# Attention, expert layer and softplus layer on one core: nine attention steps ahead, the input split among them, and the gate in four column groups

## The chip, the cores and the metric

The kernel runs on one core of a Trainium2 chip. The metric is the device time of one execution in microseconds. PE is the matrix engine, DVE the vector engine, ACT the scalar engine, POOL the general engine, SP the engine that here only issues DMAs. The time before the change is 2075.95 us, the median of 3 runs (2073.23 to 2079.36).

## The reference, cut to what matters

All data is float32.

```python
# q, k, v: (4, 8, 576, 64)
k_p = k.reshape(B, H, 72, 8, D).mean(axis=3)          # pooling over 8 positions
v_p = v.reshape(B, H, 72, 8, D).mean(axis=3)
attn = softmax(q @ k_p.T / sqrt(D));  x = attn @ v_p  # x: (2304, 512) over all heads
P = exp(x @ w_gate - max)                             # w_gate: (512, 8)
for _ in range(8):                                    # rows, then columns, to fixed sums
    P /= P.sum(1, keepdims=True) + 1e-09
    P /= P.sum(0, keepdims=True) + 1e-09
    P *= N / E
out = sum(P[:, e:e+1] * (relu(x @ w1[e]) @ w2[e]) for e in range(8))   # w1: (8, 512, 1024)
h = out @ w_in;  y = softplus(h) @ w_out              # w_in: (512, 2048)
```

## The kernel before

**Attention** goes in 32 steps. A step takes one batch, one half of the positions (W = 288) and one pair of heads; four steps in a row (`hp` 0 to 3) complete the 512 channels of 288 tokens. For a batch and a pair of heads, k and v are pooled once (`pool_kv`: a reduction each on DVE; for the first four pairs POOL adds up v), the pooled keys are transposed (`keys_first`), and they serve two steps. `attn_step(m)` overlaps several steps: it transposes q of step m+1 (`channels_first`), issues scores, maximum and difference of step m (`softmax`), transposes the attention of a step divided earlier (`turn_attn`), lets ACT take the exponent, lets DVE and POOL divide (`divide`; in the early part one step late), multiplies with v (`mix`) and pools. In the early part, step m so transposes and mixes step m-2. The last `mix` of four also computes the gate: 288 tokens by 8 experts, four products over 128 channels each, a copy by ACT and a DMA to `lgd`.

**Experts.** The tokens come in three sets (512, 896, 896 tokens: `PAIRS`), an expert's 1024 hidden units in four blocks of 256, so there are 32 blocks for each token set. A block's first layer (`first_moe`) is a 2x2 block product by seven products of sums, after Strassen and Winograd: `b11`, `t2`, `t1`, `t4`, `t3`, `b21`, `b22` are blocks of the input or differences of such (`t_sums`), `A11` to `S4` those of the weights (`sums_w1`, on POOL). Each operand is split into a rounded part and a remainder (`split_x`, `prep_w1`, `prep_w2`: ACT rounds, POOL or DVE subtracts), and each product is three matrix products (`three`). The second layer (`second`) goes by 128 tokens. The order on each engine is that of the program: first(0), first(1), second(0), first(2), second(1) and so on. The matrices of PSUM come from eight banks that all users take in turn.

**What is put where.** The input of the first token set, 512 tokens, is complete after attention step 7, mixed at step 9. Ten attention steps (`AHEAD`) and then the differences and splits of the input are issued ahead of the first block. In them, the pooling of pairs 4 to 7 stands at steps 3, 5, 7 and 9, the sums of the first weights after step 4 and their split after step 6. The rest of attention is fed in by `hook`, which is called seven times in a `first_moe` and once for every 128 tokens of a `second`; each call is a slot. Every fifth slot, beginning with the second, issues one `attn_step`. When attention is done, the slots take the iterations on P (`side`), then the scaling of the first sums by P (`shares_to_raw`), then the conversion of the last weights from 64 bits (`from_float64`). Before block 20 everything in `side` is flushed.

Two memory pools on the right side, `ld_e` and `at_e`, serve the early steps only; the pools for the hidden layer, `h` and `z`, take their place afterwards. ACT's `za` is the copy of the first product that later sums need. All DMAs are issued by SP, in program order.

Of the kernel before, what the change touches and what calls it, by code (L numbers as in the profile page):

```python
# [9 lines left out]
F32 = mybir.dt.float32  # L10
# [9 lines left out]
def attention_moe_softplus_kernel(  # L20
# [26 lines left out]
    QP = 96  # L47
    JH = S // QP // 2
    W = JH * QP
    G = JH * 2  # L50
    STEPS = B * 2 * HP
    ITERS = 8
# [171 lines left out]
    NQ = 6  # L224
    kbd = [at_p.tile([P, 2 * SP], F32, name=f"kbd{i}", bufs=1) for i in range(NK)]
    next_kv = [0]
    AHEAD = 10
    kv_t = {}
    q_l = {}
    pooled = {}  # L230
# [1 line left out]
    to_divide = []  # L232
    to_turn = []
    to_mix = []
    xb = {}

    def kv_of(m):
# [65 lines left out]
    def softmax(m):  # L303

        ps = bank("s")
        qT = q_t.pop(m)
        kb = kbd[kv_of(m) % NK]
        for j in range(JH):
            nc.tensor.matmul(ps[:QP, j * 2 * SP:(j + 1) * 2 * SP], qT[:, j * QP:(j + 1) * QP], kb)  # L309
        sv = ps[:QP, :G * SP].rearrange("p (g s) -> p g s", g=G)  # L310
        pool = at_e if m < AHEAD and m % 3 == 2 else at_p
        mx = at_p.tile([QP, G], F32, tag="mx", name="mx")
        ex = pool.tile([QP, G, SP], F32, tag="ex", name="ex")
        s1 = ps[:QP, G * SP:G * SP + G]
        nc.vector.tensor_reduce(mx, sv, axis=AX.X, op=ALU.max)
        nc.vector.tensor_tensor(ex, sv, mx.unsqueeze(2).to_broadcast([QP, G, SP]), op=ALU.subtract)

        def exp():
            nc.scalar.activation(ex, ex, AF.Exp)

        def divide():
            sm = at_p.tile([QP, G], F32, tag="sm", name="sm")
            nc.vector.tensor_reduce(s1, ex, axis=AX.X, op=ALU.add)
            nc.vector.tensor_scalar_add(s1, s1, 1e-9)
            nc.vector.reciprocal(sm, s1)
            nc.gpsimd.tensor_tensor(ex, ex, sm.unsqueeze(2).to_broadcast([QP, G, SP]), op=ALU.mult)
            to_turn.append((m, ex))

        return exp, divide
# [11 lines left out]
    def mix():  # L341
        m, aT = to_mix.pop(0)
        hb, hp = divmod(m, HP)
        vp = pooled[kv_of(m)][1]
        px = bank("px")
        for h in range(2):
            nc.tensor.matmul(px[h * D:(h + 1) * D, :W], vp[:, h, :], aT[:, h, :])  # L347

        t0 = hb * W
        here = max(0, min(W, TP0 - t0))  # L350
        x0 = x_of(0)
        if here < W and hp == 0:
            xb[hb] = at_p.tile([P, KC, W], F32, tag="xb", name="xb")
        if here:
            nc.scalar.activation(x0[:, hp, t0:t0 + here], px[:, :here], AF.Copy, scale=1.0 / POOL)
        if here < W:
            nc.scalar.activation(xb[hb][:, hp, :], px[:, :W], AF.Copy, scale=1.0 / POOL)
        if hp == HP - 1:
            if here < W:
                nc.sync.dma_start(xd[:, :, max(0, t0 - TP0):t0 + W - TP0], xb[hb][:, :, here:])  # L360
            pg = bank("pg")
            src = x0[:, :, t0:t0 + W] if here == W else xb[hb]
            for c in range(KC):
                nc.tensor.matmul(pg[:E, :W], wg[:, c, :], src[:, c, :], start=c == 0, stop=c == KC - 1)  # L364
            lg = at_p.tile([E, W], F32, tag="lg", name="lg", bufs=1)
            nc.scalar.copy(lg, pg[:E, :W])
            half, o = divmod(t0, LT * P)
            nc.sync.dma_start(lgd[half, :, o:o + W], lg)


    pool_at = {}
    for i in range(2, B * HP):
        b, hp = divmod(i, HP)
        pool_at.setdefault(hp - 2 if b == 0 else 2 * HP * b - 5 + 2 * hp, []).append(i)
    turn_at = {}
    for m, l in pool_at.items():
        turn_at.setdefault(m + 1, []).extend(l)
    turn_at.setdefault(0, []).append(1)

    def attn_step(m, early):  # L380


        last = STEPS
        if m + 1 < last:
            channels_first(m + 1)
        if m < last:
            exp, divide = softmax(m)
        while to_turn:
            turn_attn()
        for i in turn_at.get(m, ()):  # L390
            keys_first(i)
        if m < last:
            exp()
            to_divide.append(divide)
        while len(to_divide) > (1 if early else 0):
            to_divide.pop(0)()
        while len(to_mix) > (0 if early or m >= last else 1):
            mix()
        for i in pool_at.get(m, ()):
            pool_kv(i)  # L400

    for i, pool in enumerate((ld_e, ld_e, ld_p, ld_p)):
        load_kv(pool)
# [146 lines left out]
    def first_moe(n, between):  # L550

        whi, wlo = w1_t.pop(n)
        at = h_tiles(n)
# [11 lines left out]
        a, u1 = (zpool.tile([P, tb], F32, tag="z", name=x) for x in ("za", "u1"))  # L565
        add = lambda o, x, y: nc.vector.tensor_tensor(o, x, y, op=ALU.add)  # L566
        product(pa, A11, "b11")
        nc.scalar.copy(a, pa)  # L568
        between(0)
        product(pb, S2, "t2")  # L570
        add(u1, pb, a)
        between(1)
        product(pc, S1, "t1")
# [8 lines left out]
        product(pa, A12, "b21", True)  # L582
# [178 lines left out]
    def hook(light=True):  # L761
        slot[0] += 1
        if attn_m[0] is not None:
            if slot[0] % 5 == 2:
                attn_step(attn_m[0], False)
                attn_m[0] += 1
                if attn_m[0] >= STEPS and not to_turn and not to_mix:
# [17 lines left out]
    def shares_to_raw(experts):  # L785

        for e in experts:
            for i in range(TP0 // P):
                def add(i=i, e=e):
                    a, s = acc_of(1, i), prob[:, i, e:e + 1]  # L790
                    if e == 0:
                        nc.scalar.activation(a, a, AF.Copy, scale=s)
                    else:
                        nc.vector.scalar_tensor_tensor(a, raw_of(e, i), s, a, op0=ALU.mult, op1=ALU.add)
                side.extend([add, None, None] if e else [add])

    def load_x(pair):
        o = OFF[pair] - TP0
# [4 lines left out]
        return lambda i: v[:, i]  # L803


    for m in range(AHEAD):
        attn_step(m, True)
        if m == 4:
            sums_w1(0)
        if m == 6:  # L810
            prep_w1(0)
            load_w(1, 1)
    ectx.close()
    hctx = ExitStack()
    hpool = hctx.enter_context(tc.tile_pool(name="h", bufs=2, side="right"))
    zpool = hctx.enter_context(tc.tile_pool(name="z", bufs=2, side="right"))
    tpool = None


    ta = hpool.tile([P, 2, 2, TP0 // 2], F32, tag="hhi", name="ta")  # L820
    tb = hpool.tile([P, 2, 2, TP0 // 2], F32, tag="hlo", name="tb")
    t0_of = lambda i: (ta, tb)[i // 2][:, i % 2]
    first_sums = t_sums(x_of(0), t0_of, on_pool=(2,))
    first_splits = splits("moe", x_of(0), t0_of, on_pool=(2, 4))
    first_sums[0]()
    first_splits[0]()
    for x in first_sums[1:]:
        x()
    for x in first_splits[1:]:
        x()  # L830

# [25 lines left out]
    for step, (what, n) in enumerate(todo):  # L857
# [4 lines left out]
        elif what == "first":  # L862
            f, kind, pair, u = sets[n]
            nxt = sets[n + 1] if n + 1 < len(sets) else None
            if not n or sets[n - 1][0] != f:
                xs.update(xs_next)
                xs_next.clear()
            if nxt is not None and nxt[1] == "moe":
                sums_w1(n + 1)
            if nxt is not None and nxt[0] != f:  # L870

# [30 lines left out]
                load_w(1, n + 2)  # L902
            if todo[step + 1][0] != "second":
                go_on()
                prep_w2(n)
                load_w(2, n + 1)
                while pending:
                    pending.pop(0)()
        else:
# [73 lines left out]
```

## Time and profile before

| | |
|---|---|
| median of 3 runs | 2075.95 us |
| profiled execution | 2079.37 us, its span 2076.7 us |
| PE busy | 2028.2 us, 98% of the span |
| DVE busy | 1456.5 us, 70% |
| POOL busy | 1245.6 us, 60% |
| ACT busy | 836.1 us, 40% |
| mean granted clock of PE | 0.992 of 2.4 GHz |

The profiled execution is one execution, recorded by the hardware; its span reaches from the first to the last instruction, and 2.7 us lie around it. A granted clock of 1.00 is 2.4 GHz; 1.2 GHz is the other level. Matrix products are pipelined, so the records of one after the other overlap, and the distance from start to start is what one costs in a row. A 32-bit product shows as two records, with a weight load each. Names with L are lines of the kernel.

### The profile page before, as it was taken

To read this page: it belongs to the slowest core of one execution; us is meant where nothing else is said; L and a number is where in the kernel's file an instruction comes from. 1 tells how busy PE (TensorE), PEld (TensorE's weight loads), DVE (VectorE), ACT (ScalarE), POOL (GpSimd) and SP (SyncE) were. 2 spreads that over 40 slices of the span, in tenths; PEclk is the share of its full clock that TensorE was granted. 3 is DMA by queue.
4 is the path that set the end of the run, shared out by engine and by line. 5 is a ranking of instruction groups with operands and counts; after the bars stand their busy time and mean duration, and the time that the engine had idled before them with its cause. 6 is when DMAs were issued, how large, how long until landed. Compare 5 with 4: busy or idle time off the path is not lost.

```text
span 2076.7 us, 27725 instructions
## 1 busy us (share of the span) xinstructions
PE 2028.2 (98%) x10285; PEld 1753.6 (84%) x10285; DVE 1456.5 (70%) x2531; ACT 836.1 (40%) x1607; POOL 1245.6 (60%) x1011
## 2 busy tenths in 40 slices
PE   6899999999999999999999999999999999999998
PEld 4677788877888888888888888888888888888897
DVE  7787588776677667777776776777655666767766
ACT  3455544353322332222243223222222365565565
POOL 4666689987555555666555555555555554544555
PEclk9899999999999999999999999999999999999999
DMA  6343223445222332222242222222121211121132
GB/s 178 99 133 108 86 85 109 153 139 178 76 91 82 115 109 77 92 92 82 78 151 86 87 76 77 92 82 92 56 61 61 62 51 51 61 87 51 61 114 75
DMA packets 133762, 192.00 MB, mean 92 GB/s; under 512 B 26924, under 2 KB 82940, under 8 KB 133628
## 3 DMA queue, kind: packets, MB, share of 16 engines
q1 hardware_dynamic: 133628, 190.25, 29.3%
q8 instruction: 80, 1.31, 0.3%
q14 instruction: 54, 0.44, 0.1%
HBM read 166.94 MB, written 23.27 MB: 92 GB/s over the span
## 4 chain that ended last, share of the span: by engine, by line
PE 84%; DVE 7%; ACT 3%; POOL 2%; DMA 2%; issue 2%; SPq 0%; ACTq 0%; DVEq 0%; POOLq 0%
PE py L486 42%; PE p L486 31%; PE ph L486 7%; POOL w1lo L167 1%; PE s L309 1%; PE px L347 1%; DVE c L517 1%; DMA xlod<-xl 1%; DVE kp L267 1%; PE pg L364 1%; POOL w2lo L167 1%; PE pa L337 0%; DVE vp L273 0%; DVE ln L524 0%; DVE c L522 0%
## 5 line engine op out<-in xcount | busy, mean ns | idle before, releaser
L486 PE MATMUL py<-w2hi,hhi 128*128 128x512 f32 x1440 | 566.9, 394 | 4.5 <-DVE g L642 3.2
L486 PE MATMUL py<-w2lo,hhi 128*128 128x512 f32 x1440 | 562.0, 390 | 1.9 <-POOL w2lo L167 1.9
L486 PE MATMUL py<-w2hi,hlo 128*128 128x512 f32 x1440 | 561.9, 390 | 0.0
L167 POOL TENSOR_TENSOR w1lo<-w1raw,w1hi 128x512 fp32r<-128x512 f32 (+1 forms) x216 | 253.4, 1192 | 469.7 <-ACT w1hi L198 383.7
L486 PE MATMUL p<-xhi,w1hi 128*128 128x448 f32 (+1 forms) x1344 | 460.2, 342 | 9.2 <-DVE u L566 2.9
L486 PE MATMUL p<-xhi,w1lo 128*128 128x448 f32 (+1 forms) x1344 | 457.3, 340 | 6.5 <-POOL w1lo L167 6.5
L486 PE MATMUL p<-xlo,w1hi 128*128 128x448 f32 (+1 forms) x1344 | 457.7, 341 | 1.6 <-DVE xlo L439 1.6
L642 DVE SCALAR_TENSOR_TENSOR g<-py,prob,g 128x512 f32<-128x512 f32 x482 | 360.6, 749 | 102.5 <-PE py L486 90.6
L501 ACT ACTIVATE hhi<-p 128x448 fp32r<-128x448 f32 (+1 forms) x384 | 180.4, 494 | 424.7 <-PE p L486 414.4
L167 POOL TENSOR_TENSOR w2lo<-w2raw,w2hi 128x1024 fp32r<-128x1024 f32 x120 | 289.2, 2410 | 62.2 <-ACT w2hi L211 56.7
L486 PEld LDWEIGHTS py<-w2hi,hhi 128*128 128x128 f32 x1440 | 270.7, 188 | 63.3 <-DVE g L642 3.5
L486 PEld LDWEIGHTS py<-w2hi,hlo 128*128 128x128 f32 x1440 | 270.6, 188 | 59.1
L486 PEld LDWEIGHTS py<-w2lo,hhi 128*128 128x128 f32 x1440 | 271.0, 188 | 51.9 <-POOL w2lo L167 2.3
L486 PEld LDWEIGHTS p<-xhi,w1hi 128*128 128x128 f32 x1344 | 256.8, 191 | 38.7 <-DVE p L566 4.1
L486 PEld LDWEIGHTS p<-xhi,w1lo 128*128 128x128 f32 x1344 | 256.7, 191 | 20.9 <-POOL w1lo L167 8.0
L486 PEld LDWEIGHTS p<-xlo,w1hi 128*128 128x128 f32 x1344 | 256.8, 191 | 20.7 <-DVE xlo L439 2.0
L568 ACT COPY za<-p 128x448 f32<-128x448 f32 (+1 forms) x96 | 46.0, 479 | 493.0 <-PE p L486 490.7
L167 POOL TENSOR_TENSOR w1lo<-sums,w1hi 128x1024 fp32r<-128x1024 f32 x96 | 232.1, 2417 | 0.0
L502 DVE SCALAR_TENSOR_TENSOR hlo<-p,hhi 128x448 fp32r<-128x448 f32 (+1 forms) x384 | 210.7, 550 | 27.7 <-ACT hhi L501 26.8
L566 DVE TENSOR_TENSOR za<-p,za 128x448 f32<-128x448 f32 (+1 forms) x96 | 53.4, 556 | 170.1 <-PE p L486 169.7
L529 POOL TENSOR_TENSOR hlo<-ln,hhi 128x448 fp32r<-128x448 f32 (+1 forms) x96 | 100.0, 1046 | 55.1 <-ACT hhi L528 52.6
L486 PE MATMUL ph<-xhi,w1hi 128*128 128x448 f32 (+1 forms) x384 | 130.1, 339 | 0.0
(124 smaller groups left out, 2710.4 us busy)
## 6 DMA issues: line engine op xcount, KB each, us to landing
w1raw<-in_moe_w_dram SPq DMA_DIRECT2D x96, 512.0 KB
w2raw<-in_moe_w_dram SPq DMA_DIRECT2D x96, 512.0 KB
w1raw<-v SPq DMA_DIRECT2D x24, 512.0 KB
w2raw<-v SPq DMA_DIRECT2D x24, 512.0 KB
f<-in_moe_w_in_dram SPq DMA_DIRECT2D x16, 512.0 KB
v<-dt SPq DMA_DIRECT2D x32, 256.0 KB
f<-in_moe_w_out_dram SPq DMA_DIRECT2D x16, 512.0 KB
xlod<-xl SPq DMA_DIRECT2D x28, 224.0 KB
```

What stands on the lines that cost most here:

```text
L167: nc.gpsimd.tensor_tensor(o, a, b, op=ALU.subtract)
L267: nc.vector.tensor_reduce(kp, kt.rearrange("p h t d -> p h d t"), axis=AX.X, op=ALU.add)
L309: nc.tensor.matmul(ps[:QP, j * 2 * SP:(j + 1) * 2 * SP], qT[:, j * QP:(j + 1) * QP], kb)
L347: nc.tensor.matmul(px[h * D:(h + 1) * D, :W], vp[:, h, :], aT[:, h, :])
L364: nc.tensor.matmul(pg[:E, :W], wg[:, c, :], src[:, c, :], start=c == 0, stop=c == KC - 1)
L486: nc.tensor.matmul(ps, lhs[a], rhs[b], start=first and i == 0, stop=last and i == 2, skip_group_check=goes_on,)
L501: nc.scalar.activation(hh, src, AF.Relu)
L502: nc.vector.scalar_tensor_tensor(hl, src, 0.0, hh.bitcast(F32), op0=ALU.max, op1=ALU.subtract)
L529: nc.gpsimd.tensor_tensor(hl, l, hh.bitcast(F32), op=ALU.subtract)
L566: add = lambda o, x, y: nc.vector.tensor_tensor(o, x, y, op=ALU.add)
L568: nc.scalar.copy(a, pa)
L642: nc.vector.scalar_tensor_tensor(a, py, prob[:, t, e:e + 1], a, op0=ALU.mult, op1=ALU.add)
```

## The change

- Nine attention steps ahead instead of ten. In the last of them (step 8), step 7 is divided at the start, and only step 6 is transposed and mixed. Step 7 is transposed and mixed inside the first block (`early_steps_end`), behind its products `b11` and `t1`.
- Pairs 4 to 7 are pooled at steps 5, 6, 9 and 10 instead of 3, 5, 7 and 9. From step 9 on, pooled keys are transposed at a slot of their own (`to_key`).
- Among the early steps: the sums of the first weights after step 3, their split and the next load after step 4; `b11` and the second-layer weights of block 0 split after step 5; `b21` split and the weight sums of block 1 after step 6; the difference for `t1` and its split after step 7. The other differences and splits stand in `early_steps_end`. The differences lie in the second accumulator's memory (`t_in(1, 0)`) instead of tiles of the hidden layer. POOL takes the remainders of `b11`, `t1`, `t3` and `b21`; before, those of `t1` and `t3`.
- The gate is computed one step later than the mix that completes its tokens, ahead of the transposes of that step, as four groups of 72 tokens that write to partitions 0, 32, 64 and 96, and copied in four pieces.
- Later attention steps come every fourth slot, from slot 12 on.
- The scaling of the first sums takes two slots a piece instead of three.

The diff, cut to its core:

```diff
+    GQ = W // 4
-    AHEAD = 10
+    AHEAD = 9
+    FROM = 8
-        pool = at_e if m < AHEAD and m % 3 == 2 else at_p
+        pool = at_e if m < AHEAD and m % 3 == 1 else at_p
...
-            pg = bank("pg")
-            src = x0[:, :, t0:t0 + W] if here == W else xb[hb]
-            for c in range(KC):
-                nc.tensor.matmul(pg[:E, :W], wg[:, c, :], src[:, c, :], start=c == 0, stop=c == KC - 1)
-            lg = at_p.tile([E, W], F32, tag="lg", name="lg", bufs=1)
-            nc.scalar.copy(lg, pg[:E, :W])
-            half, o = divmod(t0, LT * P)
-            nc.sync.dma_start(lgd[half, :, o:o + W], lg)
+            to_gate.append((t0, x0[:, :, t0:t0 + W] if here == W else xb[hb]))
+    def gate():
+        t0, src = to_gate.pop(0)
+        pg = bank("pg")
+        for c in range(KC):
+            for j in range(4):
+                nc.tensor.matmul(
+                    pg[32 * j:32 * j + E, :GQ], wg[:, c, :], src[:, c, j * GQ:(j + 1) * GQ],
+                    start=c == 0, stop=c == KC - 1,
+                )
+        lg = at_p.tile([E, W], F32, tag="lg", name="lg", bufs=1)
+        for j in range(4):
+            nc.scalar.copy(lg[:, j * GQ:(j + 1) * GQ], pg[32 * j:32 * j + E, :GQ])
+        half, o = divmod(t0, LT * P)
+        nc.sync.dma_start(lgd[half, :, o:o + W], lg)
...
-        pool_at.setdefault(hp - 2 if b == 0 else 2 * HP * b - 5 + 2 * hp, []).append(i)
+        at = hp - 2 if b == 0 else (5, 6, AHEAD, AHEAD + 1)[hp] if b == 1 else 2 * HP * b - 5 + 2 * hp
+        pool_at.setdefault(at, []).append(i)
...
     def attn_step(m, early):
         last = STEPS
+        if m == AHEAD - 1:
+            to_divide.pop(0)()
         if m + 1 < last:
             channels_first(m + 1)
         if m < last:
             exp, divide = softmax(m)
-        while to_turn:
+        while to_gate:
+            gate()
+        while len(to_turn) > (1 if m == AHEAD - 1 else 0):
             turn_attn()
...
     def first_moe(n, between):
...
         product(pa, A11, "b11")
+        if n == 0:
+            product(pc, S1, "t1")
+            early_steps_end()
+        at = h_tiles(n)
         nc.scalar.copy(a, pa)
         between(0)
+        if n == 0:
+            product(pa, A12, "b21", True)
         product(pb, S2, "t2")
         add(u1, pb, a)
...
     def hook(light=True):
         slot[0] += 1
         if attn_m[0] is not None:
-            if slot[0] % 5 == 2:
+            if slot[0] % 4 == 2:
+                while to_key:
+                    keys_first(to_key.pop(0))
+            if slot[0] > FROM and slot[0] % 4 == 0:
                 attn_step(attn_m[0], False)
...
-                side.extend([add, None, None] if e else [add])
+                side.extend([add, None] if e else [add])
...
+    sum1, sum3, sum2, sum4 = t_sums(x_of(0), t0_of, on_pool=(2,))
+    split_b11, split_t2, split_t1, split_t4, split_t3, split_b21, split_b22 = splits(
+        "moe", x_of(0), t0_of, on_pool=(0, 2, 4, 5)
+    )
     for m in range(AHEAD):
         attn_step(m, True)
+        if m == 3:
+            sums_w1(0)
         if m == 4:
-            sums_w1(0)
-        if m == 6:
             prep_w1(0)
             load_w(1, 1)
+        if m == 5:
+            split_b11()
+            prep_w2(0)
+            load_w(2, 1)
+        if m == 6:
+            split_b21()
+            sums_w1(1)
+        if m == 7:
+            sum1()
+            split_t1()
+    def early_steps_end():
+        nonlocal hpool, zpool
+        turn_attn()
+        mix()
+        ectx.close()
+        hpool = hctx.enter_context(tc.tile_pool(name="h", bufs=2, side="right"))
+        zpool = hctx.enter_context(tc.tile_pool(name="z", bufs=2, side="right"))
+        for x in (sum3, sum2, split_t2, sum4, split_t4, split_t3, split_b22):
+            x()
```

## Rows read from the trace of the kernel before

**Rows 1.** Busy time by stretch: length, PE, PEld, DVE, ACT, POOL; clock; DMA.

```profile
0.00:57.30 57.30, 38.87 (x196) 24.52 (x196) 43.90 (x73) 23.16 (x56) 27.91 (x41) 0.94 0.65 167
57.30:88.80 31.50, 24.98 (x143) 21.37 (x144) 23.32 (x44) 13.98 (x33) 18.77 (x17) 0.73 0.31 86
```

**Rows 2.** Instructions in order of time, PE: start, length, [idle before, what ended it].

```profile
25.12 0.90 PE L309 MATMUL s<-kbd,qT 128*96 128x144 f32 x6
...
32.36 1.18 PE L337 MATMUL pa<-ident,ex 96*72 96x96 f32 x6 [3.10 <-POOL ex L326]
...
38.83 0.90 PE L309 MATMUL s<-kbd,qT 128*96 128x144 f32 x6
...
50.86 0.90 PE L309 MATMUL s<-kbd,qT 128*96 128x144 f32 x6
...
57.32 0.38 PE L486 MATMUL p<-xhi,w1hi 128*128 128x256 f32 x1 [1.00 <-ACT xhi L435]
```

**Rows 3.** Groups by line, DVE, 0 to 57.3: count, busy us, mean ns.

```profile
L267 DVE TENSOR_REDUCE kp<-kt 72x128 f32<-72x1024 f32 x8 | 15.1, 1892 | 5.2 <-DMA kt<-in_k_dram 5.2
```

**Rows 4.** In order of time, POOL, the early steps.

```profile
31.40 0.91 POOL L326 TENSOR_TENSOR ex<-ex,sm 96x432 f32<-96x432 f32 x1 [5.31 <-DVE sm L325]
32.27 0.72 POOL L164 TENSOR_TENSOR sums<-w1raw 128x256 f32<-128x256 f32 x1
...
43.44 1.96 POOL L167 TENSOR_TENSOR w1lo<-w1raw,w1hi 128x512 fp32r<-128x512 f32 x2
45.36 2.37 POOL L167 TENSOR_TENSOR w1lo<-sums,w1hi 128x1024 fp32r<-128x1024 f32 x1
```

**Rows 5.** In order of time, DVE, ACT and POOL, the first input splits.

```profile
57.61 0.67 DVE L424 TENSOR_TENSOR ta<-g 128x512 f32<-128x512 f32 x1
...
59.52 1.14 ACT L435 CAST xhi<-ta 128x512 fp32r<-128x512 f32 x2 [2.25 <-DVE ta L424]
...
60.74 1.29 POOL L439 TENSOR_TENSOR xlo<-ta,xhi 128x512 fp32r<-128x512 f32 x1 [4.17 <-ACT xhi L435]
...
61.21 1.36 DVE L439 TENSOR_TENSOR xlo<-tb,xhi 128x512 fp32r<-128x512 f32 x1 [0.35 <-ACT xhi L435]
```

**Rows 6.** The chain that ended last, in order of time: start, length, what.

```profile
77.27 3.07 POOL w1lo L167 x2
...
80.38 5.07 PE p L486 x22
...
88.99 1.39 PE py L486 x6
...
313.25 4.31 PE p L486 x36
...
330.71 4.11 PE py L486 x18
```

**Rows 7.** In order of time, PE, one attention step among expert products.

```profile
102.66 0.41 PE L286 MATMUL pq<-ident,qt 96*128 96x96 f32 x3
102.91 0.90 PE L309 MATMUL s<-kbd,qT 128*96 128x144 f32 x6
...
105.23 0.38 PE L486 MATMUL p<-xhi,w1hi 128*128 128x256 f32 x1
```

**Rows 8.** In order of time, PE, px records and the last gate.

```profile
87.38 0.46 PE L347 MATMUL px<-aT,vp 72*64 72x288 f32 x2 [0.23 <-ACT aT L338]
...
246.34 2.11 PE L364 MATMUL pg<-xb,wg 128*8 128x288 f32 x8
```

**Rows 9.** Instructions on tile pg, 246 to 249: ns min/median/max, first and last start.

```profile
L364 PEld LDWEIGHTS pg<-xb,wg x8: 86/90/90, 246.3 to 247.8; 128*8 128x8 f32 x8
L364 PE MATMUL pg<-xb,wg x8: 406/406/410, 246.3 to 248.0; 128*8 128x288 f32 x8
```

**Rows 10.** Instructions of line 660, columns as above.

```profile
L660 ACT COPY prob<-pt x2: 220/222/224, 258.2 to 258.4; 128x72 f32<-128x72 f32 x2
```

**Rows 11.** Busy time by stretch, columns as in the first group.

```profile
102.66:188.75 86.09, 84.03 (x564) 68.42 (x562) 70.66 (x138) 44.95 (x106) 54.36 (x47) 1.00 0.44 129
```

More of the change, by code (lines that the diff above doesn't have):

```diff
@@ L234, in attention_moe_softplus_kernel @@
     to_mix = []
+    to_gate = []
     xb = {}
@@ L373, in attention_moe_softplus_kernel @@
         b, hp = divmod(i, HP)
-        pool_at.setdefault(hp - 2 if b == 0 else 2 * HP * b - 5 + 2 * hp, []).append(i)
+        at = hp - 2 if b == 0 else (5, 6, AHEAD, AHEAD + 1)[hp] if b == 1 else 2 * HP * b - 5 + 2 * hp
+        pool_at.setdefault(at, []).append(i)
+    to_key = []
     turn_at = {}
     for m, l in pool_at.items():
-        turn_at.setdefault(m + 1, []).extend(l)
+        if m < AHEAD:
+            turn_at.setdefault(m + 1, []).extend(l)
     turn_at.setdefault(0, []).append(1)
@@ L400, in attn_step @@
             pool_kv(i)
+            if m >= AHEAD:
+                to_key.append(i)
     for i, pool in enumerate((ld_e, ld_e, ld_p, ld_p)):
@@ L552, in first_moe @@
         whi, wlo = w1_t.pop(n)
-        at = h_tiles(n)
         def product(ps, a, b, onto=False):
@@ L564, in first_moe @@
         pa, pb, pc, pd = (bank(f"p{x}", "p")[:, :tb] for x in "1654")
-        a, u1 = (zpool.tile([P, tb], F32, tag="z", name=x) for x in ("za", "u1"))
         add = lambda o, x, y: nc.vector.tensor_tensor(o, x, y, op=ALU.add)
         product(pa, A11, "b11")
+        if n == 0:
+            product(pc, S1, "t1")
+            early_steps_end()
+        at = h_tiles(n)
+        a, u1 = (zpool.tile([P, tb], F32, tag="z", name=x) for x in ("za", "u1"))
         nc.scalar.copy(a, pa)
         between(0)
+        if n == 0:
+            product(pa, A12, "b21", True)
         product(pb, S2, "t2")
@@ L572, in first_moe @@
         between(1)
-        product(pc, S1, "t1")
+        if n:
+            product(pc, S1, "t1")
         between(2)
@@ L581, in first_moe @@
         between(4)
-        product(pa, A12, "b21", True)
+        if n:
+            product(pa, A12, "b21", True)
         between(5)
@@ L763, in hook @@
         if attn_m[0] is not None:
-            if slot[0] % 5 == 2:
+            if slot[0] % 4 == 2:
+                while to_key:
+                    keys_first(to_key.pop(0))
+            if slot[0] > FROM and slot[0] % 4 == 0:
                 attn_step(attn_m[0], False)
                 attn_m[0] += 1
-                if attn_m[0] >= STEPS and not to_turn and not to_mix:
+                if attn_m[0] >= STEPS and not to_turn and not to_mix and not to_gate:
                     attn_m[0] = None
@@ L803, in t_in @@
         return lambda i: v[:, i]
+    hctx = ExitStack()
+    hpool = zpool = tpool = None
+    t0_of = t_in(1, 0)
+    sum1, sum3, sum2, sum4 = t_sums(x_of(0), t0_of, on_pool=(2,))
+    split_b11, split_t2, split_t1, split_t4, split_t3, split_b21, split_b22 = splits(
+        "moe", x_of(0), t0_of, on_pool=(0, 2, 4, 5)
+    )
     for m in range(AHEAD):
         attn_step(m, True)
+        if m == 3:
+            sums_w1(0)
         if m == 4:
-            sums_w1(0)
-        if m == 6:
             prep_w1(0)
             load_w(1, 1)
[L813 to L830, printed above, removed]
+        if m == 5:
[17 more added lines that the diff above has]
+            x()
+        xs.update(xs_next)
+        xs_next.clear()
     todo = []
@@ L867, in attention_moe_softplus_kernel @@
                 xs_next.clear()
-            if nxt is not None and nxt[1] == "moe":
+            if nxt is not None and nxt[1] == "moe" and ("s", n + 1) not in raw_t:
                 sums_w1(n + 1)
@@ L904, in attention_moe_softplus_kernel @@
                 go_on()
-                prep_w2(n)
-                load_w(2, n + 1)
+                if n not in w2_t:
+                    prep_w2(n)
+                    load_w(2, n + 1)
                 while pending:
```

## The prediction

> **What bounds the kernel now.** I read the busy time by stretch first. The matrix engine (PE) is at work for 98% of the whole span, but the early stretches differ: up to 57.3 us it is busy 38.87 us, with DVE the busiest engine (43.90), and from 57.3 to 88.8 it is busy 24.98 of 31.50 us at a mean granted clock of 0.73, so a good part of that ran at 1.2 GHz instead of 2.4 [rows 1]. What can be won by reordering lies there; later only what makes PE do less, or wait more, counts.
>
> Then the order of PE's work. The score product of step 4 starts at 25.12, that of step 6 at 38.83, of step 9 at 50.86, the first expert product at 57.32 [rows 2]. In between PE waits 3.10 us for POOL's division of step 3 [rows 2]. POOL itself had been idle for 5.31 us before that division, waiting for DVE's reciprocal [rows 4], and DVE was pooling: a kp reduction takes 1.89 us and vp has the same shape [rows 3]. So DVE's pooling sets these steps, and POOL's queue comes next.
>
> Last the chain of waits after 57.3. PE waits behind POOL's remainders of the second weight set (3.07 us), and then 22 products need 5.07 us where 36 need 4.31 later: the lower clock follows the wait [rows 6]. So the second set is interrupted until the first down-projection at 88.99 [rows 6].
>
> **Prices.** A small expert product costs 4.31/36 = 0.120 us, a wide one 4.11/18 = 0.228 [rows 6]. A block is 42 small products (5.03 us, 7 slots), its second layer 24 wide ones (5.48 us, 4 slots): 0.955 us a slot without attention. One attention step put between them costs 105.23 - 102.66 = 2.57 us of PE [rows 7].
>
> **1. The early steps.** Pairs 4 and 5 are pooled at steps 5 and 6 instead of 3 and 5, pairs 6 and 7 after the early part: DVE loses four reductions, 7.6 us [rows 3]. With no pooling at step 3, DVE takes step 4's scores when they are there, at 26, not behind two reductions. POOL is late next, since it gets work earlier: sums of set 0 after step 3 (4 x 0.72), remainders of w1 after step 4 (1.96 + 2.37), of w2 after step 5 (2.4, same shape), sums of set 1 after step 6 (2.9) [rows 4], and three input remainders (b11, b21, t1) at 1.29 each [rows 5]. With the divisions of steps 3 to 7 at 0.91 [rows 4] that is 2.9 + 4.3 + 2.4 + 2.9 + 3.9 + 4.6 = 21.0 us in one queue from 26 on, so step 7's division is done at 47 to 48. Behind each such block stands a division, and behind that PE's transposes of two steps later; I put the last early transposes (step 6) at 45.6, the mix after them until 47.5, and the first expert product there. Ends: if every step took only PE's 2.57, step 8 would start at 25.12 + 4 x 2.57 = 35.4 and the product some 5 us later, 40; at the old mean pitch (25.12 to 50.86, five steps, 5.15) it is 51. I take 47.5, since the POOL sum is made of rows. On SP the weights of set 1 are asked for earlier; each load waits for POOL to free its buffer, and the q loads queued behind are six steps ahead, which covers them; without that cover a late q would hold the next step's first transposes.
>
> **2. Inside the first block.** Products b11 and t1 run at once. Then PE needs `za`, a copy that ACT reaches only after everything in early_steps_end: aT, x, and four roundings, with DVE's differences and remainders between them. After step 7's mix (about 52) I add: x copy 0.6, difference 1.2 beside POOL, rounding 0.6, remainder 0.9, difference 0.67, three roundings 1.7, `za` 0.4 [rows 5]: 6 us, `za` at about 57.8. PE idles until then. The 30 products left take between 30 x 0.12 = 3.6 and 30 x 0.23 = 6.9 us (the 22 that took 5.07 [rows 6]), depending on the clock: 5.3, block done at 63.
>
> **3. The second block.** Its sums and weights are ready before, and prep_w1(1) waits only for ACT: w1's remainders (4.3) about 60 to 64.3, as PE reaches them. I allow 1.5 us of wait. With 36 products (4.3) and step 9 (slot 12) the first down-projection starts at 63 + 4.3 + 2.6 + 1.5 = 71.4. Before: 88.8, with steps up to 12 done. That is 17.4 earlier, with three steps, 7.7, still owed: **-9.7 us**. With part 1 at its ends this is -17 to -6.
>
> **4. The gate.** Eight records over 288 columns take 2.11 us [rows 8]. Four column groups make 32 records of 72 columns. If the groups run side by side, 8 rounds are bound by 72/288 x 0.26 = 0.07 or by the weight load, 0.09 [rows 9]: 0.72, with a tail about 0.9. If they don't, 32 x 0.083 (three transposes start within 0.25 [rows 7]) = 2.7. Ends 0.5 and 2.7; I take 0.9: a gate record lasts 0.41 from start to end [rows 9], and two in a row would need 0.65, but two px records of the same length in columns, which go to two column groups, are done within 0.46 [rows 8]. ACT now copies four pieces (a 72-column copy takes 0.22 [rows 10]; chained, about 0.6 in all) ahead of the aT copies for which PE waits: 0.35 us a gate given back. Net -1.2 + 0.45 = -0.75 for each of 6 gates among the expert products, **-4.5 us** (ends -9 and +7). The early two lie in part 1.
>
> The Trainium skill speaks against this edit: TensorE: Matmul & The Clock Gate (Part 1, "Wait — 56ns, not 53.3ns?") gives about 62 ns per matmul as the bound of short ones where the sequencer's own code decodes them. By it 32 records take 1.98 us and this term shrinks to about +1, an estimate from that page, 2072 in all. Two px records within 0.46 us start closer than that, so the trace doesn't agree [rows 8]; what chance it has lies in (c) below.
>
> **5. Steps every fourth slot.** 11 steps and 55 slots take 86.09 us with DVE busy 70.66 [rows 11]: 7.83 a step, 6.42 of DVE. A slot less takes away about 0.53 of DVE (hlo, sums and accumulation; estimate) and 0.955 of PE, the cheaper gate 0.15: DVE 5.9 of 6.7 us, 88% instead of 82%. PE idled 2.06 of 86.09 [rows 11]; I allow +1.5 over 24 steps. Steps 9, 10 and 11 each pool a pair, 3.8 us: 8.7 of DVE in 6.7, 6 us too much in 20, which the banks partly take up: +2.5. Ends 0 and +14. **+4 us**.
>
> **6. The end of attention.** It ends at slot 108 (one more call, for the last gate) instead of 112; the shares take 28 slots, not 40, with DVE denser there, and the weight conversion starts some 16 slots earlier. PE does the same work: **+0.5 us** (-1 to +2).
>
> Sum: -9.7 - 4.5 + 4 + 0.5 = -9.7. The profiled execution took 2079.37 us (span 2076.7 and 2.7 around it): 2069.7. The median of the runs is 2075.95, 3.4 lower, so 2066.2: I say **2066**.
>
> **Rivals.** (a) POOL's queue is less in the way than I count, its pieces falling into PE's waits: product at 43, `za` 2 us sooner; 6 us more, 2060. For it: POOL's added work stands in a stretch where it waited for DVE (5.31 at once [rows 4]). Against it: nearly all of it falls into 25 us.
> (b) The early part slips: POOL's blocks add to DVE's poolings at steps 5 and 6 instead of hiding behind them, product near 51, the low clock lasts longer: -6 in place of -9.7, and +6 for part 5: 2072. For it: the clock of 0.73 after such waits [rows 1].
> (c) The gate doesn't run in groups, the records follow one another at the transposes' spacing: 2.7 instead of 2.1 and 0.35 of copies, +5.7 in place of -4.5, 2076. For it: 72-column records are not in the trace. Against it: px [rows 8].
> (d) Slower: DVE becomes the bound between slots 12 and 108. It is one queue; kp and vp hold it 3.8 us, and hlo and the accumulation that free PE's operands and banks stand behind. A period of 6.7 that grows by 0.4 on each of 24 steps uses up the gain; by 0.9 it is +12 net, 2088. For it: 82% busy already [rows 11]. Against it: at 82% PE lost 2.4%.
>
> **How the numbers follow.** Forecast 0.48, (a) 0.20, (b) 0.20, (c) 0.04, (d) 0.08. A difference under 0.3%, 6.2 us, is about what can't be told from no change: faster means below 2069.7. The forecast's own spread (2061 to 2071) leaves 0.06 of its chance above that. Faster 0.42 + 0.20 = 0.62; same 0.06 + 0.20 + 0.04 = 0.30; slower 0.08. Range 2055 to 2077: it takes in (a), (b) and (c) and leaves out (d) and the far ends.
>
> **What would show it.** First expert product near 47.5 and first down-projection near 71 (part 1 wrong if after 51, part 3 if the latter is past 76). A PE gap of some 5 us ended by ACT's `za` in the first block. Gate records of about 0.9 us together, several starting at once. PE waits on DVE around slots 12 to 24 of a few us, DVE near 88% until pooling ends. Last gate near 235 instead of 246.34 [rows 8], and from there the two profiles at the same distance. The prediction is wrong if that distance changes by several us later, or if PE idles more than 5% between slots 24 and 108.

## The result and the profile after

The changed kernel takes 2089.48 us (median of 6 runs, 2087.53 to 2092.57) against 2075.05 for the kernel before (6 runs): a ratio of 1.0063 [1.0050, 1.0077], about 13 us slower. The prediction was 2066, with 0.08 on slower. The profiled execution took 2089.57 us, its span 2087.8, 11.1 longer than before (the profiled execution of before, 2079.37, was the slowest of its six runs).

First the order of PE's work after: start, length, what, in brackets the idle time before it and what ended it.

```profile
48.57 0.58 PE L508 MATMUL p<-xhi,w1hi 128*128 128x256 f32 x1
...
59.57 0.58 PE L508 MATMUL p<-xhi,w1hi 128*128 128x256 f32 x1 [5.40 <-ACT za L593]
...
71.08 0.69 PE L372 MATMUL pg<-xb,wg 128*8 128x72 f32 x32
...
76.37 0.25 PE L298 MATMUL pk<-ident,kp 72*128 72x72 f32 x1 [3.69 <-DVE kp L270]
76.51 0.47 PE L508 MATMUL py<-w2hi,hhi 128*128 128x512 f32 x1
...
257.60 0.69 PE L372 MATMUL pg<-xb,wg 128*8 128x72 f32 x32
```

The first down-projection (`py`, the second layer) before:

```profile
88.83 0.39 PE L486 MATMUL py<-w2hi,hhi 128*128 128x512 f32 x1
```

The first expert product starts at 48.57 where it was 57.32 [rows 2], the first down-projection at 76.51 where it was 88.83 (the 88.99 of [rows 6] isn't the first): so far the change is ahead. The last gate starts at 257.60 where it was 246.34 [rows 8]: now it is 11.3 behind. From there to the end both run equally long (2087.8 - 257.60 = 1830.2; 2076.7 - 246.34 = 1830.4). The net loss lies between the first down-projection and the last gate.

That stretch in one row for each kernel: length, busy time of PE, PEld, DVE, ACT and POOL with counts, granted clock, DMA share, GB/s. After:

```profile
76.51:257.60 181.09, 164.36 (x1176) 133.65 (x1175) 129.23 (x250) 89.95 (x224) 103.74 (x94) 0.93 0.38 108
```

Before:

```profile
88.80:246.34 157.54, 153.33 (x1016) 122.99 (x1014) 115.31 (x231) 83.63 (x196) 103.33 (x92) 1.00 0.37 110
```

It is 23.6 us longer. Three steps owed from the early part are 3 x 2.57 = 7.7 [rows 7], and five gates at 0.69 instead of 2.11 [rows 8] take away 7.1. The last gate stands at slot 108 instead of 112, so the stretch also holds 24 small products fewer, 2.9 us at 0.120. So some 26 us are new. The rows say what they are: PE is idle for 181.09 - 164.36 = 16.7 us instead of 4.2, 12.5 more, and its clock is 0.93 instead of 1.00, which is worth up to 0.07 x 181 = 12.7 us of work ("up to", since part of the low clock falls into the waits). POOL has no more to do, ACT 6 us.

What PE waited for from 76.3 to 215, by when all pairs are pooled (waiter, what it waited for, us in total, times, longest):

```profile
PE pk L298 <- DVE kp L270: 16.8, 10, 3.7
...
PE px L350 <- ACT aT L341: 0.6, 1, 0.6
```

One line is nearly all of it: the transposes of `pk` (in keys_first), which read the pooled keys `kp`. The first of the ten waits, 3.69 us, ends just ahead of the stretch in the row; the nine in it take 13.1 us, 2.2 at most, and all other idle time there is 3.6 us. Before, their seven records in this stretch have no such wait. How the first one comes about, on DVE, in order of time:

```profile
71.33 0.59 DVE L318 TENSOR_REDUCE mx<-s 96x6 f32<-96x432 f32 x1
71.95 0.60 DVE L319 TENSOR_TENSOR ex<-s,mx 96x432 f32<-96x432 f32 x1
72.48 0.60 DVE L326 TENSOR_REDUCE s<-ex 96x6 f32<-96x432 f32 x1
...
74.34 1.88 DVE L270 TENSOR_REDUCE kp<-kt 72x128 f32<-72x1024 f32 x1
76.14 1.97 DVE L276 TENSOR_REDUCE vp<-vt 72x128 f32<-72x1024 f32 x1
```

The attention step gives DVE the softmax of its scores and, behind that, the pooling of a pair. Two slots later PE's queue holds that pair's key transposes. PE reaches them at 72.68 and stands until `kp` is done at 76.2, while the down-projection stands behind them, its hidden values complete since 68.0 (the last of their remainders, `hlo`, on DVE). The same two views show the second half of the price, PE before and after that wait:

```profile
72.03 0.28 PE L508 MATMUL p<-xhi,w1lo 128*128 128x256 f32 x1
72.16 0.28 PE L508 MATMUL p<-xhi,w1hi 128*128 128x256 f32 x1
72.28 0.29 PE L508 MATMUL p<-xlo,w1hi 128*128 128x256 f32 x1
...
76.82 0.39 PE L508 MATMUL py<-w2lo,hhi 128*128 128x512 f32 x1
77.04 0.39 PE L508 MATMUL py<-w2hi,hlo 128*128 128x512 f32 x1
...
78.29 0.41 PE L508 MATMUL p<-xhi,w1hi 128*128 128x256 f32 x1
78.51 0.42 PE L508 MATMUL p<-xlo,w1hi 128*128 128x256 f32 x1
78.72 0.41 PE L508 MATMUL p<-xhi,w1lo 128*128 128x256 f32 x1
```

Before the wait one small product follows another after 0.12 us, after it every 0.21: the lower of the two clock levels, 1.2 GHz. It doesn't set in at once (two down-projections at 76.82 and 77.04 still start 0.22 apart); from 77.5 to 80.9 the granted clock is 0.51, so the wait of 3.69 us costs some 1.7 us more. Four of the nine waits in the stretch, those of 1.8 to 2.2 us, are followed by such a spell too; the last spell, at 251.6, follows a wait of 1.05 us for `aT`, so not all of the low clock belongs to `kp`.

And the gate, records on tile pg from 70 to 73 (ns minimum, median, maximum; first and last start):

```profile
L372 PE MATMUL pg<-xb,wg x32: 225/226/229, 71.1 to 71.5; 128*8 128x72 f32 x32
...
L378 ACT COPY lg<-pg x4: 207/210/213, 71.8 to 72.5; 8x72 f32<-8x72 f32 x4
```

### The profile page after: what moved, and what is told of

Same layout as the page of the kernel before. It is cut to its first block, busy times and chain, and to the rows that moved or that the text cites. A ratio compares the mean times of both kernels' runs of the same rounds, so it can differ in the third digit from the quotient of the medians.

```text
span 2087.8 us, 28158 instructions
## 1 busy us (share of the span) xinstructions
PE 2026.0 (97%) x10477; PEld 1758.0 (84%) x10477; DVE 1454.3 (70%) x2529; ACT 839.3 (40%) x1631; POOL 1247.6 (60%) x1013
## 4 chain that ended last, share of the span: by engine, by line
PE 85%; DVE 8%; ACT 3%; issue 1%; POOL 1%; DMA 1%; SPq 0%; ACTq 0%; DVEq 0%; POOLq 0%
PE py L508 43%; PE p L508 32%; PE ph L508 7%; DVE kp L270 1%; PE s L312 1%; PE px L350 1%; DVE c L539 1%; PE pa L340 1%; DVE ln L546 0%; DVE c L544 0%; ACT xhi L457 0%; DVE vp L276 0%; DVE s L326 0%; ACT ln L540 0%; DVE g L656 0%
## 5 line engine op out<-in xcount | busy, mean ns | idle before, releaser
L508 PEld LDWEIGHTS py<-w2lo,hhi 128*128 128x128 f32 x1440 | 271.8, 189 | 51.9 <-POOL w2lo L168 2.3
```

Of the source, the lines that this page charges most:

```text
L508: nc.tensor.matmul(ps, lhs[a], rhs[b], start=first and i == 0, stop=last and i == 2, skip_group_check=goes_on,)
```

## The experiments

The theory was: the loss is PE waiting, in order, for DVE's pooling, since `keys_first` now stands too close behind `pool_kv` and `pool_kv` stands ahead of work that PE needs. The rival was (d): with a step every fourth slot there is too much work for DVE, wherever it stands. Ratios are to the kernel before, run on the same chip; 0.0005 is about 1 us. The labels e1 to e14 are those that the recorded expectations use.

**Key transposes later, nothing else (e1, e2).** First moved to just before the next step, four slots behind the pooling; then, for pairs 8 on, to six slots.

```diff
-            if slot[0] % 4 == 2:
+            if slot[0] > FROM and slot[0] % 4 == 0:
                 while to_key:
                     keys_first(to_key.pop(0))
-            if slot[0] > FROM and slot[0] % 4 == 0:
                 attn_step(attn_m[0], False)
```

> The changed kernel with one edit: the pooled keys are transposed just ahead of the next attention step, four slots after their pooling, instead of two. Theory (late keys): PE's key transposes stand in its queue two slots after the pooling and wait there for DVE's kp reduction, 20.5 us in all by the trace, and the clock falls after each wait, some 10 us more. Then the waits of pk on kp fall below 5 us, the mean clock between 76 and 262 us is at least 0.97, and the time is 2058 to 2069 us. Rival (DVE is full): an attention step every four slots asks more of DVE than there is, so the wait moves to hlo, the accumulation or the scores, and the time stays at 2083 to 2092 us.

```diff
-                while to_key:
-                    keys_first(to_key.pop(0))
+                while to_key and (to_key[0][0] < 2 * HP or attn_m[0] - to_key[0][1] >= 2):
+                    keys_first(to_key.pop(0)[0])
```

> The changed kernel with the keys of pairs 8 on transposed one attention period later, six slots after their pooling (pairs 6 and 7 stay at two slots, since the next step needs them). Late keys: only the waits of pairs 6 and 7 stay, about 4 to 6 us; 2058 to 2069 us, beside the run with four slots. DVE is full: 2083 to 2092 us, as there.

Measured: 1.0052 [1.0033, 1.0072] and 1.0042 [1.0026, 1.0057], so 2 and 4 us better than the change as it was, far less than the 16.8 us of waits (the 20.5 of the expectation counts the first wait twice). Both times, 2086.49 and 2085.07, lie in the rival's range and not in the theory's. The waits of PE from 76.3 to 215 with six slots:

```profile
PE p L508 <- DVE u L586: 3.5, 1, 3.5
PE p L508 <- DVE p L586: 3.4, 1, 3.4
PE py L508 <- ACT xb L360: 1.3, 1, 1.3
```

The nine waits for `kp` are down to one of 0.4 us, and two others have come. Pair 6's wait, 3.7 us at 74.81, stays, since its keys were left at two slots; the waits up to 76 have it:

```profile
PE pk L298 <- DVE kp L270: 4.1, 2, 3.7
```

DVE just before the wait for `u`:

```profile
156.48 1.86 DVE L270 TENSOR_REDUCE kp<-kt 72x128 f32<-72x1024 f32 x1
158.26 1.86 DVE L276 TENSOR_REDUCE vp<-vt 72x128 f32<-72x1024 f32 x1
```

Its product on PE:

```profile
160.51 0.52 PE L508 MATMUL p<-xhi,w1hi 128*128 128x256 f32 x1 [3.50 <-DVE u L586]
```

A pooling that falls on the first slots of an expert block holds up for 3.7 us the sums (`u`, `p`) that the block's next products read. So the theory had a second half: where in the block the pooling falls.

**The same distance in the kernel before (e3).** Keys of pairs 8 to 15 two slots behind the pooling, steps still every fifth slot.

```diff
...
+            if m >= AHEAD:
+                to_key.append(i)
...
+            if slot[0] % 5 == 4:
+                while to_key:
+                    keys_first(to_key.pop(0))
```

> The kernel before with one edit: for pairs 8 to 15 the keys are transposed two slots after the attention step that pools them, instead of in the next step, five slots after. Steps stay at every fifth slot. Late keys: eight waits of about 2 us and the clock after them make it slower, 2087 to 2097 us. DVE is full: DVE has room at five slots, so nothing changes, 2072 to 2079 us.

1.0039 [1.0024, 1.0054]: this alone makes the kernel before 8 us slower; 2083.3 lies between the two ranges. Only four of the eight pairs wait for their keys from 88 to 250, and their 4.4 us are about half of the loss:

```profile
PE pk L295 <- DVE kp L267: 4.4, 4, 3.1
```

**The gate alone (e4)**, in the kernel before, called where the old gate stood, its copy in four pieces as in the change.

```diff
             for c in range(KC):
-                nc.tensor.matmul(pg[:E, :W], wg[:, c, :], src[:, c, :], start=c == 0, stop=c == KC - 1)
+                for j in range(4):
+                    nc.tensor.matmul(pg[32 * j:32 * j + E, :GQ], wg[:, c, :], src[:, c, j * GQ:(j + 1) * GQ], start=c == 0, stop=c == KC - 1)
...
```

> The kernel before with the gate alone as four column groups and four copies, at its old place at the end of a mix. In the changed kernel 32 records take 0.69 us where eight took 2.11. If PE's time counts there, the gate gives 1.4 us for each of eight gates less up to 0.3 for ACT's copies: 2064 to 2068 us. If it was hidden beside another wait: 2073 to 2077 us.

0.9979 [0.9968, 0.9990], 4.4 us faster; the median, 2071.87, lies between the two ranges, and the span is 6.6 shorter. From first down-projection to last gate it takes 155.4 instead of 157.5 us, not the 7 less that five gates give: PE now waits 3.9 us in five places for ACT's `xb`, the input of the gate, which the longer gates had covered but for 0.2.

**Poolings behind the sums (e5).** On top of six slots: a pooling due in the first four slots of a block waits until behind the sums.

```diff
+            if m >= AHEAD and place[0] < 4:
+                to_pool.append((i, m))
+                continue
...
         place[0] = k
         hook()
+        if k == 4:
+            while to_pool:
+                pool_kv(to_pool[0][0])
+                to_key.append(to_pool.pop(0))
```

> The changed kernel with late keys (as in e2), and where a step that pools falls on one of the first four slots of a block, its pooling is issued at the fifth slot, behind the block's own sums on DVE. Theory (place): PE stalls 3.5 us where kp and vp (3.8 us) stand on DVE ahead of the sums u, za and p that the next expert products wait for, and then runs at the low clock for a while; the two such stalls and their clock go: 2071 to 2077 us, and no wait of p on u or p over 1.5 us between 76 and 215. Rival (density): at four slots a step DVE is late everywhere, the waits move to hlo, the accumulation or the division: 2082 to 2088 us as e2.

1.0033 [1.0022, 1.0044], 2 us better than without, which the intervals don't tell from nothing; 2082.37 lies in the rival's range. The stalls on `u` and `p` are gone from 76 to 215, as the theory said, but between 76 and 170 PE still waits for `kp` three times, 7.2 us in all: a deferred pooling is closer to its keys, and pairs 6 and 7 still have two slots.

**Every fifth slot (e6, e6b)**, with six slots for the keys, from slot 19 (meant to put all poolings on good places) and from slot 12.

```diff
...
-            if slot[0] > FROM and slot[0] % 4 == 0:
+            if slot[0] >= 19 and (slot[0] - 19) % 5 == 0:
...
```

> The changed kernel with late keys, attention steps every fifth slot from slot 19 on: the steps that pool fall on the same slots of a block as in the kernel before (the 11th, 10th, down to the fourth). Density and place both expect the early gain to stay: 2062 to 2070 us.

> As e6 but from slot 12 on: the same distance of five slots, with four of the eight later poolings on the first four slots of a block. Place: four stalls of 2 to 3.5 us and the clock after them, 10 to 18 us slower than e6, 2074 to 2086. Density: the same as e6 within 4 us.

1.0026 [1.0015, 1.0037] and 1.0053 [1.0038, 1.0068]. The old pitch doesn't win the loss back, against both theories, which had expected 2062 to 2070 of the first (2080.41). At one pitch the two starts differ by 5.6 us, between what place and density had asked for; place isn't the only difference, since one begins seven slots later. The first was no clean "good" either: pair 6's pooling fell on slot 0 of its block, and in the profiled execution, the slowest of seven, PE waited 4.3 us for `u` and 3.9 for `kp` before 125.

**`za` first (e8).** On top of six slots, the `za` copy ahead of the last input splits (`last_splits` is the loop that ended `early_steps_end`).

```diff
             early_steps_end()
         at = h_tiles(n)
...
         nc.scalar.copy(a, pa)
+        if n == 0:
+            last_splits()
```

> The changed kernel with late keys (as in e2), and ACT's copy za issued before the last input splits instead of behind them. The trace has PE waiting 5.4 us for za. Theory: about 2.5 us of it go, since b21 runs at once and PE then waits for t2's split; 2081 to 2084 us against e2's 2085. Rival: the first products' end is set by the last splits in any case, so nothing changes beyond 1 us.

1.0042 [1.0028, 1.0056], as without it, as the rival said. The wait for `za` falls from 5.4 to 1.0 us, and nothing is won. The rows from 45 to 76.5 say where it went, the change as it was (its program is that of e2 up to there) and then `za` first:

```profile
45.00:76.50 31.50, 20.41 (x140) 17.09 (x141) 15.93 (x33) 13.87 (x34) 15.65 (x15) 0.70 0.10 27
45.00:76.50 31.50, 24.15 (x141) 19.79 (x142) 16.07 (x33) 13.64 (x34) 16.22 (x16) 0.61 0.10 27
```

PE is busy for 3.7 us more with the same records, at a lower clock: the second block begins 2.0 us sooner (63.58 instead of 65.58), but its first 16 products start every 0.21 us where they had started every 0.12. From the first expert product to the first down-projection it takes 27.7 us, against 26.7 to 27.9 in the four versions without this edit that start at 48.3 to 48.6.

**Pairs 6 and 7 pooled at steps 7 and 8 alone (e9a), and then all three places together (e9b):** the pairs early, poolings behind the sums, keys six slots behind the pooling itself or when the next step needs them. The pitch is four slots in both. The second extract shows only the keys' line, against e5; e9b has the edits of e5 and e9a as well.

```diff
-        at = hp - 2 if b == 0 else (5, 6, AHEAD, AHEAD + 1)[hp] if b == 1 else 2 * HP * b - 5 + 2 * hp
+        at = hp - 2 if b == 0 else (5, 6, 7, 8)[hp] if b == 1 else 2 * HP * b - 5 + 2 * hp
```

> The changed kernel with one edit: pairs 6 and 7 are pooled in the early part, at steps 7 and 8, as the kernel before pools all of pairs 4 to 7 there, instead of at steps 9 and 10. Theory (bunched pooling): steps 9, 10 and 11 each pool a pair, and the key waits of pairs 6 and 7 (3.7 and 3.7 us in the trace of the changed kernel or its variants) with the low clock after them cost some 10 us; the early part gets 2 to 4 us longer: 2081 to 2085 us. Rival: the early part grows by as much as is saved, since DVE has no room there: 2087 to 2092.

```diff
...
-                while to_key and (to_key[0][0] < 2 * HP or attn_m[0] - to_key[0][1] >= 2):
+                while to_key and (slot[0] - to_key[0][1] >= 6 or kv_of(attn_m[0]) == to_key[0][0]):
```

> Three edits on the changed kernel: pairs 6 and 7 pooled early (e9a), poolings kept off the first four slots of a block (e5), and keys transposed six slots after their pooling, or when the next step needs them. Theory (place of the poolings and keys): all long waits of PE on kp, u and p between 76 and 215 us go and the clock stays at 1.00, so the early gain and the gate's remain: 2065 to 2073 us. Rival (density): at four slots a step other waits come up, 2077 to 2083.

1.0032 [1.0019, 1.0045] and 0.9987 [0.9976, 0.9997]. The pairs early give back 6.4 us by themselves, in the theory's range, though not for its reasons alone: pair 7's keys wait for 0.45 us in the change, not 3.7. The three together give back 16 us and make the change 2.7 us faster than the kernel before; their 2074.45 lies between the two ranges. From first down-projection to last gate:

```profile
75.50:242.58 167.08, 158.70 (x1173) 128.58 (x1173) 124.03 (x250) 92.20 (x229) 106.46 (x96) 0.97 0.38 110
```

Nearly the same instructions of PE in 14 us less than after: idle 8.4 instead of 16.7 us, clock 0.97 instead of 0.93. DVE has 5.2 us less to do there, since pairs 6 and 7 are pooled earlier. Its longest waits of PE from 76.3 to 215:

```profile
PE pa L340 <- DVE hlo L529: 1.4, 1, 1.4
PE px L350 <- DVE hlo L529: 1.0, 2, 0.6
PE s L312 <- DVE hlo L529: 1.0, 1, 1.0
```

DVE in one and the same stretch, after and then with the three places:

```profile
76.50:215.00 138.50, 122.81 (x881) 99.92 (x881) 106.65 (x198) 66.61 (x168) 71.88 (x66) 0.93 0.41 114
```

```profile
76.50:215.00 138.50, 131.17 (x986) 106.96 (x985) 110.57 (x218) 75.91 (x189) 86.70 (x79) 0.98 0.40 113
```

DVE does more in the better kernel, 110.57 against 106.65 us, and PE loses less. So in the change, at 77%, DVE wasn't at its limit.

**Two of the places taken back from that kernel:** the keys two slots behind the pooling again (e12), and the poolings not deferred (e13).

```diff
-                while to_key and (slot[0] - to_key[0][1] >= 6 or kv_of(attn_m[0]) == to_key[0][0]):
+                while to_key:
```

> e9b with one of its three edits taken back: the keys are transposed at the first free slot of their kind again, two slots after a pooling at a step (one to three after a deferred one). Theory (late keys): with the poolings well placed and pairs 6 and 7 early, eight key waits of 1 to 4 us come back, with the low clock after them: 6 to 14 us slower than e9b, 2080 to 2088. Rival: moving the keys only moves the wait, as the small gain of e1 and e2 suggests: within 3 us of e9b.

```diff
-            if m >= AHEAD and place[0] < 4:
-                to_pool.append((i, m))
-                continue
```

> e9b with another of its edits taken back: poolings are issued in the step that owns them wherever it falls, so four of eight fall on the first four slots of a block. Place: two stalls of about 3.5 us on u and p and the clock after them come back, 4 to 9 us slower than e9b, 2078 to 2083. Rival: within 2 us.

1.0041 [1.0026, 1.0057] and 1.0039 [1.0027, 1.0051]: 11 us lost by each (9 by the medians), as the theory of places said or a little more. Pitch and DVE's work are those of e9b, so here it is the order alone. The waits from 76.3 to 215 are the two kinds seen above, each by itself. Keys close behind:

```profile
PE pk L298 <- DVE kp L270: 10.4, 6, 3.1
```

Poolings not deferred:

```profile
PE p L510 <- DVE u L588: 3.5, 1, 3.5
PE p L510 <- DVE p L588: 3.4, 1, 3.4
```

**Further versions.** All three places with steps every fifth slot (e10); with `za` first (e11); with both (e14).

```diff
-            if slot[0] % 4 == 2:
+            if slot[0] % 5 == 0:
...
-            if slot[0] > FROM and slot[0] % 4 == 0:
+            if slot[0] >= 12 and slot[0] % 5 == 2:
```

> As e9b with an attention step every fifth slot instead of every fourth. Place: within 3 us of e9b. Density: 6 to 10 us faster than e9b.

> As e9b with ACT's copy za issued before the last input splits. PE's wait for za was 5.4 us and 1.0 with this edit in e8, whose first down-projection yet came no sooner. Theory: the last splits set the end of the first block, nothing is gained beyond 1 us. Rival: in e8 the gain was lost to the wait on pair 6's keys just behind, which is gone here: 1.5 to 3 us faster than e9b.

> The best version so far (e10, five slots) with za first: 2068 to 2071 us; if the za copy gives nothing, as e10, 2071.

0.9979 [0.9969, 0.9989], 0.9983 [0.9975, 0.9992] and 1.0004 [0.9994, 1.0014]. The fifth slot gains 1.7 us on the fourth, with intervals that overlap (place had said within 3, density 6 to 10), and `za` first, added to the fourth, gains nothing that can be told. Both edits together lose 5 us against the fifth slot alone, outside both expectations. In the profiles 4.4 us of it are there at the first down-projection (78.13 against 73.78) and 3.2 at the first expert product (54.17 against 51.00), where the two programs are still the same. So that part can't be told from the scatter of the early part: in five versions whose program is the same up to there (e9a, e9b, e10, e12, e13) the product starts between 51.0 and 54.3. The clock differs too (fifth slot alone, then with `za` first):

```profile
45.00:76.50 31.50, 21.54 (x156) 18.45 (x157) 22.47 (x42) 14.12 (x35) 14.14 (x14) 0.75 0.25 70
```

```profile
45.00:76.50 31.50, 21.71 (x106) 17.77 (x110) 21.15 (x36) 11.73 (x28) 14.57 (x13) 0.62 0.24 65
```

Why the early part differs from one execution to the next stays open. The best version beats the kernel before by 4.4 us, no more than the gate alone does.

## Why the prediction was wrong

**The step that failed is part 5,** with the key transposes in their own slot, which part 5 never priced: +4, with bounds 0 and +14. Measured are some 26 us in the stretch, 12.5 of them more idle time of PE and the rest its lower clock, which mostly follows these waits; 3.69 more of waiting come just ahead of it. Part 5 added up DVE's work over three periods ("6 us too much in 20") and let the banks absorb it (five pairs are pooled in [rows 11], so by its own rows a step that pools takes some 8.0 us of DVE, not 8.7, and the excess is 4, not 6). It didn't ask which instruction of PE stands right behind each pooling. `keys_first` had been issued one whole step, five slots, behind `pool_kv`; the diff has it two slots behind, 1.9 us of PE, and the pooling that it reads ends behind a softmax and a 1.89 us reduction [rows 3]. That could be read from the diff and the rows of before. The prediction asked what DVE's queue delays, not what PE's queue is made to wait for. Its own marks say so: PE idles 16.7/181.1 = 9% where more than 5% was to refute it, and DVE, put near 88%, is busy for 77%.

**Rival (d) had the sign and the size, 2088, but not the mechanism.** It had DVE full and each of 24 periods 0.9 longer. With the pitch unchanged, moving three things gave back 16 us, and two of them taken back singly, with all of DVE's work kept, cost 11 each. The third, pairs 6 and 7 early, takes DVE work out of the dense steps 9 to 11; it gave back 6.4 us alone, and how much of that is place and how much is density isn't shown. It wasn't taken back alone either: the kernel with poolings behind the sums, which lacks it and counts the keys' distance from the step and not from the pooling, is 9.5 slower. The effects don't add up to the whole: six slots for the keys took away all but 0.4 us of nine waits for `kp`, and two waits of 3.4 and 3.5 us for `p` and `u` came in their place.

**Parts 1 to 3** were right in kind. The first expert product came at 48.57 (47.5 predicted); the `za` gap is 5.40 us ("some 5"), ending at 59.57 (57.8 predicted). The first down-projection came at 76.51, past the 76 at which the prediction called part 3 wrong; 3.69 of the 5.1 us too many are again part 5's wait, for pair 6's `kp`. Instead of -9.7 the three parts gave -12.3 + 7.7 = -4.6. The `za` gap, although of the predicted size, wasn't worth anything: with it gone PE does the same products at a lower clock, and the time is the same.

**Part 4** was right: 0.69 us against 0.9 predicted, and the gate alone makes the kernel 4.4 us faster (-4.5 predicted, for six gates), though by another account. Its first down-projection is 2.6 us earlier already (86.25 against 88.83); the two early gates, which the prediction left out of this term, may be the reason, but e3, unchanged up to there, was 1.3 earlier too. From there each gate saves 1.4, not 1.2, but the wait for `xb`, which wasn't foreseen, takes 3.9 of the 7.1 back. That the total met the forecast is in part luck. Rival (c) is out. The 62 ns per matmul, which the Trainium skill's page TensorE: Matmul & The Clock Gate (Part 1, "Wait — 56ns, not 53.3ns?") gives where the sequencer's own code decodes them, are no bound here: the 32 records start (0.69 - 0.226)/31 = 15 ns apart on average, and counted as the program's 16 products 31 ns.

**Part 6** was right by its mark: the distance from the last gate to the end is the same within 0.2 us, although it now holds the 24 products (2.9 us) and a gate that is 1.4 cheaper; what takes up the 1.5 stays open. Rivals (a) and (b) ask about the early part: it came at 48.57, neither at 43 nor at 51. But that is one execution: in the six versions with the same program up to there it came four times at 48.3 to 48.4 and twice at 51.7 to 51.9, near (b).

With the places right, the rest of the change (earlier experts, denser steps) nets about nothing: all three places together stand 1.7 us behind the gate alone, with intervals that overlap. How much of the clock each single wait cost, and why the version with five slots and `za` first is slower, stays open. The kernel before with the gate in groups and its poolings deferred as well wasn't tried.

## What to carry to other kernels

When an edit moves a consumer on an in-order engine, go through the pairs: for each moved instruction, how much of the consumer's engine lies between it and its producer, and what stands ahead of the producer in its own queue. A busy share can't answer that: DVE was at 77% in the slower kernel and at 80% in the faster one. And try repairs together as well as singly: added one at a time they gave back 2 to 6 us each, together 16, and two of them cost 11 each when taken out of the good version.

## What the runs showed of the hardware

Short matmuls in four column groups ran side by side: 32 records of 72 columns take 0.69 us, 3.1 times faster than eight of 288 at 2.11 [rows 8], although a record alone lasts 0.226.

PE held to its order: one transpose of 72 columns, for which `kp` was missing, kept down-projections, whose hidden values were complete, waiting for 3.69 us. The Trainium skill, TensorE: Matmul & The Clock Gate (Part 3, "The mechanism", under "What overlaps and what doesn't") says that matmuls start and end in program order; the trace agrees.

Nine waits for `kp` in 181 us, 1.5 us in the mean and 2.2 at most, and one of 3.69 just before them went with a granted clock of 0.93 in place of 1.00. PE at 1.2 GHz cost about as much again (up to 12.7 us) as the idle time that was added (12.5). Five of the six spells stand behind such waits, one behind a wait of 1.05 us for `aT`.

A wait taken away isn't a gain by itself: with `za` first PE waited 4.4 us less between 45 and 76.5 and was busy 3.7 us more with the same records, at a granted clock of 0.61 in place of 0.70.
